# Attention and a mixture of experts on one core: score tiles in goes of six, one accumulator bank per half of d

## The chip, the cores and the metric

The kernel runs on one core of a Trainium2 chip. The core has a matrix engine (TensorE, PE in the profile, its weight loads on a row of their own, PEld), a vector engine (VectorE, DVE), a scalar engine (ScalarE, ACT), GpSimd (POOL) and SyncE (SP), which issues most transfers. TensorE writes into PSUM: eight banks, each holding 512 float32 values in each of 128 partitions. ScalarE and VectorE read the banks. The metric is the time of one execution on the device in microseconds.

## The reference

Attention without softmax over 8 batches of 2496 rows, then routing to 8 experts with a fixed capacity, then a two-layer expert network.

```python
scores = (1.0 / S) * np.matmul(z, z.transpose(0, 2, 1))   # z: 8 x 2496 x 64
attn = np.maximum(scores, 0.0) ** 2
out = u * np.matmul(attn, v)                              # u, v: 8 x 2496 x 256
x = out.reshape(B * S, D)
logits = x @ w_gate                                       # 8 experts
# (token, expert) pairs in falling order of their logit; a pair is taken
# if the token is free and the expert has room for N/8 = 2496 tokens
h = np.maximum(x[mask] @ w1[e], 0.0)                      # 256 -> 1024
out[mask] = h @ w2[e]                                     # 1024 -> 256
```

## The kernel before

**Precision.** Matmuls take float32 values as a rounded part (hi, h) and a remainder (lo, l). A product is three matmuls: hi·hi, hi·lo and lo·hi. So `zh`/`zl`, `vh`/`vl`, `hi`/`lo`, `w1h`/`w1l`, `xh`/`xl` and `hh`/`hl` are such pairs: the first part is copied by ScalarE as a rule, the remainder subtracted by VectorE.

**Attention: groups and steps.** A batch has 2496 rows: 19 key tiles of 128 and one of 64 (KT = 20). Queries are taken in five groups g of 512 columns (the last has 448). For each (batch b, group g, key tile kt) there is one step n, 800 in all (`seq`). The loop at L1016 writes out one step after another. In a step it issues, in this order: a go of scores when one is due, Relu (`rectify`, ScalarE) of the tile four steps ahead (LA = 4), square (`square`, ScalarE) of the tile two ahead, the remainder (`split_lo`, VectorE) of the next tile, the rounded part (`split_hi`; three of five on ScalarE, two on VectorE) of the tile two ahead, the output matmuls (`av`) of this step's tile, and what the table `todo` holds for this step.

**Scores.** z's columns have 64 rows, so two 64-row matmuls for two key tiles run side by side in two halves of the array, three products each (L825, the six-matmul *pair*). A *go* is the score tiles issued one after another in one step: four tiles, two pairs, at every fourth step. Each tile takes a bank of the ring `sc`, which has SCB = 4 banks. The ring also serves the transposes of z for the next batch (`z_turn`, L786, one bank, read by `zh` L792 and `zl` L793), and of the output (`turn_back`, L891, two banks, read by `post_mul` L902).

**Output.** `av` adds the products of attn and v to two banks `acc0`, `acc1`, one for each half d of v's 256 columns. Each has two buffers, so the eight banks are four for scores and four for accumulators. After a group's last tile, `take_acc` copies both into `at0` (ScalarE, L879) and `at1` (VectorE, L877) as work of the table at step m0, the next group's first. Two steps later `turn_back` turns them, one more later `post_mul` multiplies by u and stores x, and then 32 logit products (`post_logits`, L919) per group are spread on VectorE over 13 steps.

**Next batch.** z is turned 60 steps ahead of a batch, one `z_turn` every four steps; v is split (`split_v`, L806, L807) one tile per step during the last group of the batch before.

**A planner** orders each engine's instructions before the run: it takes them as written, earlier ones first, but puts a later one ahead where, by its own costs, the earlier one's inputs or buffer aren't there yet. On the chip each engine then keeps this order.

**Second stage.** Experts are taken in an order found while running; for each, a list of its 2496 rows is made (`route`, VectorE mainly), rows are gathered (`gather_x`, GpSimd), turned (`turn_x`, `xp`, L541, L550, L551) and put through both layers (L557 to L559, L588 to L590), and scattered (`put_y`, L621). An expert has 40 steps (5 groups of 8, PER = 40). While one expert is computed, the list of the next is made in pieces: `advance` is called twice a step and deals out the list's pieces evenly. With AHEAD = 10, list k starts 10 steps before expert k-1 and must be done 10 steps before expert k, when its first gather is written (list 1 starts somewhat later). Weights of an expert are split (`split_w`, L509, L511) from ten steps before it.

Of the kernel before, what the change touches and what calls it, by code (L numbers as in the profile page):

```python
# [107 lines left out]
def moe(tc, xd, first, jp, identf, w1, w2, out, B, S, cp):  # L108
# [18 lines left out]
    PLANS = ((4, 3, 3, 3, 3), (3, 3, 3, 3, 2, 2))  # L127
    ND = 15
    LA = 3
    AHEAD = 10  # L130
    YIELDS = 88
    with ExitStack() as ctx:
        rp = ctx.enter_context(tc.tile_pool(name="rp", bufs=1))
# [498 lines left out]
        def at(n, f, *a):  # L632
            todo.setdefault(n, []).append((f, a))

        for k in range(E):
            for g in range(NG):
                n0 = (k * NG + g) * FT
                at(1 if (k, g) == (0, 1) else n0 - 12 if g else n0 - AHEAD, gather_x, k, g)
                if (k, g) == (0, 0):
                    at(n0 - 6, turn_x, k, g, range(DH))  # L640
                else:
                    for d in range(DH):
                        at(n0 - 4 if (k, g) == (0, 1) else n0 - 6 + d, turn_x, k, g, (d,))
# [13 lines left out]
        steps_k = {k: 0 for k in range(E)}  # L657
        gens = {k: route(k) for k in range(1, E)}

        def advance(pos):  # L660
            k = pos // (2 * PER) + 1
            if k >= E:
                return
            skip = 2 * (AHEAD - 3) if k == 1 else 0
            if pos < skip:
                return
            want = -(-(pos % (2 * PER) - skip + 1) * YIELDS // (2 * PER - skip))
            if (pos + 1) % (2 * PER) == 0:
                want = 1000
            while steps_k[k] < want:  # L670
                w = next(gens[k], "end")
                if w == "end":
                    break
                steps_k[k] += w if isinstance(w, (int, float)) else 1
# [17 lines left out]
def attention(tc, u, v, z, w_gate, xd, identf, made, first, scale):  # L692
# [11 lines left out]
    JP = lg.shape[1]  # L704
    LA = 4
    RING = KT + 2
    SCB = 4
    with ExitStack() as ctx:
        io = ctx.enter_context(tc.tile_pool(name="io", bufs=3))
        zp = ctx.enter_context(tc.tile_pool(name="zp", bufs=2))  # L710
# [6 lines left out]
        def load_gate():  # L717
            wgb = wk.tile([128, E, D], F32, name="wgb", bufs=1)
            for h in range(2):
                wg = wk.tile([128, DH, 128 * E // 2], F32, name="wg", tag="xs")  # L720
                wg = wg.rearrange("p a b -> p (a b)")
                nc.sync.dma_start(wg, bass.AP(tensor=w_gate.tensor, offset=w_gate.offset + h * 128 * E,
                                              ap=[[0, 128], [1, 128 * E]]))
                with in_turn(0):
                    nc.vector.tensor_copy(wgb[:, :, h * 128:(h + 1) * 128], wg.rearrange("p (d e) -> p e d", e=E))
            wgt = wk.tile([128, DH, E], F32, name="wgt", bufs=1)
            nc.sync.dma_start(wgt, w_gate.rearrange("(h p) e -> p h e", h=DH))
            WG.update(rows=wgb, cols=wgt)
# [83 lines left out]
        def width(g):  # L812
            return min(512, S - 512 * g)

        def scores(n):
            b, g, kt = seq[n]
            w = width(g)
            q = slice(g * 512, g * 512 + w)
            for m in range(0, 4, 2):
                pair = [ps.tile([128, 512], F32, name="sc", bufs=SCB)[:, :w] for _ in range(2)]  # L820
                for key, query in ((ZH, ZH), (ZH, ZL), (ZL, ZH)):
                    for s in range(2):
                        r = slice(DQ * s, DQ * s + DQ)
                        k = (kt + m + s) * 128
                        nc.tensor.matmul(pair[s], key[b][r, k:k + 128], query[b][r, q],  # L825
                                         start=key is ZH and query is ZH, stop=key is ZL)
                for s in range(2):
                    SC[n + m + s] = pair[s]

        def rectify(n):  # L830
            p = SC.pop(n)
# [2 lines left out]
            R[n] = r  # L834

        def square(n):
            a = wk.tile([128, 512], F32, name="a")[:, :width(seq[n][1])]
            nc.scalar.activation(a, R.pop(n), AF.Square)  # L838
            A[n] = a

        def split_hi(n):
            h = wk.tile([128, 512], F32R, name="hi", bufs=4)[:, :width(seq[n][1])]
            if n % 5 < 3:
                nc.scalar.activation(h, A[n], AF.Copy)  # L844
            else:
                nc.vector.tensor_copy(h, A[n])
            HI[n] = h

        def split_lo(n):
            a, h = A.pop(n), HI[n]  # L850
            if seq[n][2] == NT:
                nc.vector.tensor_sub(h[TL:], a[TL:], h[TL:].bitcast(F32))
                return
            l = wk.tile([128, 512], F32R, name="lo", bufs=4)[:, :width(seq[n][1])]
            recent["l"] = nc.vector.tensor_sub(l, a, h.bitcast(F32))  # L855
            LO[n] = l

        def av(n):
            b, g, kt = seq[n]
            if kt == 0:  # L860
                ACC[b, g] = [ps.tile([128, 512], F32, name=f"acc{d}") for d in range(2)]
            last = kt == NT
            h, l = HI.pop(n), LO.pop(n, None)
            for d in range(2):
                o = ACC[b, g][d][:, :width(g)]
                c = slice(d * 128, (d + 1) * 128)
                vh, vl = VH[b, kt][:, c], VL[b, kt][:, c]
                nc.tensor.matmul(o, vh, h, start=(kt == 0), stop=False)  # L868
                if not last:
                    nc.tensor.matmul(o, vh, l, start=False, stop=False)  # L870
                nc.tensor.matmul(o, vl, h, start=False, stop=last)  # L871

        def take_acc(b, g, d):
            t = wk.tile([128, 512], F32, name=f"at{d}", bufs=2)[:, :width(g)]
            o = ACC[b, g][d][:, :width(g)]
            if d:
                nc.vector.tensor_copy(t, o)  # L877
            else:
                nc.scalar.activation(t, o, AF.Copy)  # L879
            AT[b, g, d] = t  # L880
# [12 lines left out]

        def post_mul(b, g, half):
            if half == 0:
                XS[b, g] = wk.tile([128, 4, D], F32, name="xs")
            acc = ACC[b, g][half].rearrange("p (i d) -> p i d", d=D)
            full = NT - 4 * g - 2 * half
            cuts = [(0, 2, 128)] if full >= 2 or b % 2 else [(0, full, 128), (full, 2, TL)]
            for i, j, n in cuts:  # L900
                c = slice(2 * half + i, 2 * half + j)
                nc.vector.tensor_mul(XS[b, g][:n, c], acc[:n, i:j], UR[b, g][:n, c])  # L902
            if half == 1:
                xs = XS[b, g]
                n = min(4, NT - 4 * g)
                nc.sync.dma_start(xd[b * S:b * S + NT * 128].rearrange("(p i) d -> p i d", i=NT)[:, 4 * g:4 * g + n],
                                  xs[:, :n])
                if n < 4:
                    nc.sync.dma_start(xd[b * S + NT * 128:(b + 1) * S], xs[TL * (b % 2):TL * (b % 2) + TL, n])
# [12 lines left out]
        def last_logits(b, g):  # L922
            xs = XS[b, g]
            p = ps.tile([128, 512], F32, name="sc", bufs=SCB)
            xt = [wk.tile([128, 512], F32, name="xt", tag=t, bufs=n) for t, n in (("r", 4), ("a", 3))]
            for d in range(DH):
                t = ps.tile([128, 512], F32, name="sc", bufs=SCB)
                for i in range(4):
# [22 lines left out]
        def premask(lo, hi):  # L951
            at_least(nc, first["mask0"], first["rep"], first["at0"], lo, hi)

        todo = {}

        def at(n, f, *a):
            todo.setdefault(n, []).append((f, a))
# [7 lines left out]
        for b in range(B):  # L965
            for g in range(NQ):
                n0 = (b * NQ + g) * KT
                m0 = n0 + KT
                t = m0 + (0 if m0 == B * NQ * KT else 2)
                for d in range(2):  # L970
                    at(m0, take_acc, b, g, d)
                at(t, turn_back, b, g)
                for d in range(2):
                    at(t + 1, post_mul, b, g, d)
# [9 lines left out]
            if b:  # L984
                for g in range(NQ):
                    m = n0 - 3 * KT + 4 * g
                    at(m - 4, load_z, b, g)
                    at(m, z_turn, b, g)
                    at(n0 - KT + 4 * g - 8, load_v, b, g)
                at(n0 - 3 * KT + 4 * NQ + 2, swap_z, b, slice(0, KT * 128))  # L990
                for kt in range(KT):
                    at(n0 - KT + kt, split_v, b, kt)
            else:
                for kt in range(KT):
                    at(kt - 4, split_v, 0, kt)
# [16 lines left out]
            early.enter_context(tc.issue_after(i.ins))  # L1012
        at(14, load_gate)
        N = len(seq)
        start = min(min(todo), -LA)
        for n in range(-LA, N + 4 * E):  # L1016
            if n == 2:
                early.close()
            if n % 4 == 0 and 0 <= n + LA < N:
                scores(n + LA)  # L1020
            if 0 <= n + LA < N:
                rectify(n + LA)
            if 0 <= n + 2 < N:
                square(n + 2)
            if 0 <= n + 1 < N:
                split_lo(n + 1)
            if 0 <= n + 2 < N:
                split_hi(n + 2)
            for k in sorted(k for k in todo if k < n):
# [31 lines left out]
```

## Time and profile before

| what | us |
|---|---|
| median of three runs | 2611.67 (2609.31 to 2612.87) |
| the profiled execution | 2615.43 |
| its span, first to last instruction | 2613.3 |
| attention ends (last output matmul into a bank) | about 1479 |
| first list and first gather, TensorE mostly idle | 1481 to 1560 |
| second stage, TensorE busy again | 1560 to 2614 |

The profile is of one execution. It lists for each engine the busy time, in stretches of the span too; for each group of instructions count, busy time and mean; and, in the timeline, start, duration, engine, line, operation, output<-inputs and count of merged neighbours, with the idle time before and what ended it in square brackets. A matmul's row shows its time from entering to leaving; since matmuls are pipelined the next one starts earlier. `acc<-hi,vh 128*128` is an output matmul on the whole array, `sc<-zh 64*128` a score matmul on half of it.

### The profile page before, as it was taken

To read this page: it belongs to the slowest core of one execution; us is meant where nothing else is said; L and a number is where in the kernel's file an instruction comes from. 1 tells how busy PE (TensorE), PEld (TensorE's weight loads), DVE (VectorE), ACT (ScalarE), POOL (GpSimd) and SP (SyncE) were. 2 spreads that over 40 slices of the span, in tenths; PEclk is the share of its full clock that TensorE was granted. 3 is DMA by queue.
4 is the path that set the end of the run, shared out by engine and by line. 5 is a ranking of instruction groups with operands and counts; after the bars stand their busy time and mean duration, and the time that the engine had idled before them with its cause. 6 is when DMAs were issued, how large, how long until landed. Compare 5 with 4: busy or idle time off the path is not lost.

```text
span 2613.3 us, 44527 instructions
## 1 busy us (share of the span) xinstructions
PE 2536.1 (97%) x16035; PEld 2088.6 (80%) x16035; DVE 1992.7 (76%) x6142; ACT 1521.8 (58%) x2941; POOL 381.6 (15%) x507
## 2 busy tenths in 40 slices
PE   9999999999999999999999859999999999999998
PEld 6777777777777777777777648888989889898997
DVE  6888788887898888887888768869696868686322
ACT  7788787787788887887877412323232323233332
POOL 2000000000000000000000003233333333333331
PEclk9999999999999999999999859999999999999999
DMA  4121120220221211211100011112121212122110
GB/s 139 41 79 48 51 69 32 63 73 19 61 72 39 65 48 41 80 48 51 39 32 25 16 41 46 62 47 69 42 69 43 68 45 67 46 82 63 46 42 24
DMA packets 71645, 139.60 MB, mean 53 GB/s; under 512 B 12160, under 2 KB 39680, under 8 KB 71424
## 3 DMA queue, kind: packets, MB, share of 16 engines
q1 hardware_dynamic: 56320, 95.84, 11.4%
q0 software_dynamic: 15104, 40.91, 4.9%
q8 instruction: 126, 2.06, 0.3%
q14 instruction: 95, 0.78, 0.1%
HBM read 85.60 MB, written 40.89 MB: 48 GB/s over the span
## 4 chain that ended last, share of the span: by engine, by line
PE 76%; DVE 19%; ACT 2%; issue 1%; DMA 1%; POOL 0%; POOLq 0%; DVEq 0%; ACTq 0%; SPq 0%
PE acc L868 13%; PE acc L871 12%; PE acc L870 11%; PE sc L825 11%; PE hp L557 4%; PE y L588 4%; PE y L590 4%; PE y L589 4%; PE hp L558 4%; PE hp L559 4%; DVE lt L919 3%; DVE ob L430 2%; DVE lo L855 2%; PE srch L241 2%; PE sc L891 1%
## 5 line engine op out<-in xcount | busy, mean ns | idle before, releaser
L855 DVE TENSOR_TENSOR lo<-a,hi 128x512 fp32r<-128x512 f32 (+1 forms) x760 | 512.3, 678 | 189.4 <-ACT hi L844 183.9
L868 PE MATMUL acc<-hi,vh 128*128 128x512 f32 (+1 forms) x1600 | 647.6, 405 | 1.7 <-ACT hi L844 1.7
L871 PE MATMUL acc<-hi,vl 128*128 128x512 f32 (+1 forms) x1600 | 619.0, 387 | 0.0
L870 PE MATMUL acc<-lo,vh 128*128 128x512 f32 (+1 forms) x1520 | 589.9, 388 | 0.4 <-DVE lo L855 0.2
L838 ACT ACTIVATE a<-r 128x512 f32<-128x512 f32 (+1 forms) x800 | 492.4, 632 | 146.9 <-DVE lo L855 146.8
L576 ACT ACTIVATE hh<-hp 128x512 fp32r<-128x512 f32 (+1 forms) x320 | 187.4, 586 | 542.3 <-PE hp L559 481.4
L919 DVE SCALAR_TENSOR_TENSOR lt<-xs,wgb 128x256 bf16<-128x256 f32 x1248 | 467.6, 423 | 0.5
L833 ACT ACTIVATE r<-sc 128x512 f32<-128x512 f32 (+1 forms) x800 | 426.5, 589 | 63.0 <-PE sc L825 60.8
L868 PEld LDWEIGHTS acc<-hi,vh 128*128 128x128 f32 x1600 | 301.4, 188 | 120.7 <-issue 38.9
L588 PE MATMUL y<-w2h,hh 128*128 128x256 f32 (+1 forms) x1280 | 366.4, 286 | 0.5 <-ACT y L615 0.5
L589 PE MATMUL y<-w2l,hh 128*128 128x256 f32 (+1 forms) x1280 | 363.3, 284 | 0.0
L871 PEld LDWEIGHTS acc<-hi,vl 128*128 128x128 f32 x1600 | 301.7, 189 | 57.1 <-issue 0.9
L870 PEld LDWEIGHTS acc<-lo,vh 128*128 128x128 f32 x1520 | 287.1, 189 | 50.4 <-DVE lo L855 4.7
L844 ACT ACTIVATE hi<-a 128x512 fp32r<-128x512 f32 (+1 forms) x480 | 292.3, 622 | 57.2 <-PE acc L871 55.3
L557 PE MATMUL hp<-xh,w1h 128*128 128x512 f32 (+2 forms) x646 | 265.0, 411 | 0.7 <-ACT xh L550 0.7
L558 PE MATMUL hp<-xl,w1h 128*128 128x512 f32 (+2 forms) x646 | 251.9, 390 | 0.0
L621 POOL DMA_INDIRECT out_dram<-y,idx x160 | 197.4, 1234 | 370.4 <-ACT y L615 323.4
L559 PE MATMUL hp<-xh,w1l 128*128 128x512 f32 (+2 forms) x646 | 250.7, 389 | 0.0
L588 PEld LDWEIGHTS y<-w2h,hh 128*128 128x128 f32 (+1 forms) x1280 | 241.0, 188 | 11.2 <-ACT y L615 0.9
L589 PEld LDWEIGHTS y<-w2l,hh 128*128 128x128 f32 (+1 forms) x1280 | 241.0, 188 | 9.3
L482 POOL DMA_INDIRECT xg<-xd,idx x160 | 165.2, 1033 | 387.3 <-PE xp L541 156.7
L216 POOL IOTA slot<- 128x256 bf16 x1 | 1.5, 1530 | 1454.8 <-DVE xs L902 1454.8
(1154 smaller groups left out, 3791.3 us busy)
## 6 DMA issues: line engine op xcount, KB each, us to landing
vr<-in_v_dram SPq DMA_DIRECT2D x32, 512.0 KB, 3.5
ur<-in_u_dram SPq DMA_DIRECT2D x32, 512.0 KB, 4.1
xd<-xs SPq DMA_DIRECT2D x32, 512.0 KB, 2.9
wr<-in_moe_w_dram SPq DMA_DIRECT2D x32, 512.0 KB, 5.2
zh<-zh SPq DMA_DIRECT2D x14, 320.0 KB, 3.4
zl<-zl SPq DMA_DIRECT2D x14, 320.0 KB, 5.2
zin<-in_z_dram SPq DMA_DIRECT2D x31, 128.0 KB, 2.0
vr<-in_v_dram SPq DMA_DIRECT2D x8, 384.0 KB, 3.1
```

The lines of the kernel that those rows point to most:

```text
L557: nc.tensor.matmul(p[:, c], wh, xh, start=(d == 0), stop=False)
L558: nc.tensor.matmul(p[:, c], wh, xl, start=False, stop=False)
L559: nc.tensor.matmul(p[:, c], wl, xh, start=False, stop=(d == DH - 1))
L588: nc.tensor.matmul(o, h[:, c], wh, start=first, stop=False, skip_group_check=True)
L589: nc.tensor.matmul(o, h[:, c], wl, start=False, stop=False, skip_group_check=True)
L833: recent["r"] = nc.scalar.activation(r, p, AF.Relu, scale=scale)
L838: nc.scalar.activation(a, R.pop(n), AF.Square)
L855: recent["l"] = nc.vector.tensor_sub(l, a, h.bitcast(F32))
L868: nc.tensor.matmul(o, vh, h, start=(kt == 0), stop=False)
L870: nc.tensor.matmul(o, vh, l, start=False, stop=False)
L871: nc.tensor.matmul(o, vl, h, start=False, stop=last)
L919: nc.vector.scalar_tensor_tensor(t[r], XS[b, g][r, i], 1.0, WG["rows"][r, e], op0=OP.mult, op1=OP.mult, accum_out=lg[r, j, e:e + 1])
```

## The change

- **Goes of six.** The ring `sc` has six banks (SCB = 6). The first 20 tiles are scored in goes of four, the others in goes of six.
- **One bank per half of d.** `acc0` and `acc1` have one buffer each. The first two and the last two key tiles of a group are taken together in the second's step: first both tiles' products for half 0, then both for half 1 (`av_half`). `take_acc` of half 0 now heads the step after the group's last; that of half 1 stands behind the step's `split_lo`. `turn_back` and what follows it move by one step where they would fall next to a go of scores.
- **v's splitting** for the next batch starts 18 steps ahead of it and takes 1.7 steps per tile, so that it runs over the last group and into the next batch; v's loads move with it.
- **More buffers** for `a` (3 to 5), `hi` and `lo` (4 to 6); fewer for `at0`, `at1` (2 to 1) and `xs` (3 to 2).
- **Second stage.** AHEAD is 12: lists from the third on, and the first gathers of experts from the third on, come two steps earlier. List 1 and its gather keep their steps (LATE = 2), so list 2 has 38 steps in place of 40.

```diff
-    AHEAD = 10
+    AHEAD = 12
+    LATE = 2
...
-                at(1 if (k, g) == (0, 1) else n0 - 12 if g else n0 - AHEAD, gather_x, k, g)
+                at(1 if (k, g) == (0, 1) else n0 - AHEAD + (LATE if (k, g) == (1, 0) else 0), gather_x, k, g)
...
+        starts = [None, 2 * (AHEAD - 3), 2 * (PER + LATE)] + [2 * PER * k for k in range(2, E)]
+
         def advance(pos):
-            k = pos // (2 * PER) + 1
-            if k >= E:
+            k = max([k for k in range(1, E) if starts[k] <= pos], default=0)
+            if k == 0 or pos >= 2 * PER * (E - 1):
                 return
-            skip = 2 * (AHEAD - 3) if k == 1 else 0
-            if pos < skip:
-                return
-            want = -(-(pos % (2 * PER) - skip + 1) * YIELDS // (2 * PER - skip))
-            if (pos + 1) % (2 * PER) == 0:
+            end = starts[k + 1] if k + 1 < E else 2 * PER * (E - 1)
+            want = -(-(pos - starts[k] + 1) * YIELDS // (end - starts[k]))
+            if pos + 1 == end:
                 want = 1000
...
-    SCB = 4
+    SCB = 6
...
-        def scores(n):
-            b, g, kt = seq[n]
-            w = width(g)
-            q = slice(g * 512, g * 512 + w)
-            for m in range(0, 4, 2):
+        def scores(first, count):
+            for n in range(first, first + count, 2):
+                b, g, kt = seq[n]
+                w = width(g)
+                q = slice(g * 512, g * 512 + w)
...
+        def av_half(n, d):
+            b, g, kt = seq[n]
+            last = kt == NT
+            o = ACC[b, g][d][:, :width(g)]
+            c = slice(d * 128, (d + 1) * 128)
+            h, l, vh, vl = HI[n], LO.get(n), VH[b, kt][:, c], VL[b, kt][:, c]
+            nc.tensor.matmul(o, vh, h, start=(kt == 0), stop=False)
+            if not last:
+                nc.tensor.matmul(o, vh, l, start=False, stop=False)
+            nc.tensor.matmul(o, vl, h, start=False, stop=last)
...
-                ACC[b, g] = [ps.tile([128, 512], F32, name=f"acc{d}") for d in range(2)]
...
+                ACC[b, g] = [ps.tile([128, 512], F32, name=f"acc{d}", bufs=1) for d in range(2)]
+            outer = kt < 2 or kt > KT - 3
+            if outer and kt % 2 == 0:
+                return
+            now = (n - 1, n) if outer else (n,)
             for d in range(2):
...
+                for i in now:
+                    av_half(i, d)
+            for i in now:
+                HI.pop(i), LO.pop(i, None)
...
-                for d in range(2):
-                    at(m0, take_acc, b, g, d)
+                while m0 < B * NQ * KT and (t + LA - KT) % 6 not in (1, 2, 3, 4):
+                    t += 1
+                ends[m0] = (b, g)
...
-                    at(n0 - KT + 4 * g - 8, load_v, b, g)
+                    at(n0 - KT - 6 + 7 * g, load_v, b, g)
...
-                    at(n0 - KT + kt, split_v, b, kt)
+                    at(n0 - KT + 2 + 17 * kt // 10, split_v, b, kt)
...
+        goes = {n: 4 for n in range(0, KT, 4)}
+        goes.update((n, SCB) for n in range(KT, N, SCB))
...
-            if n % 4 == 0 and 0 <= n + LA < N:
-                scores(n + LA)
+            if n in ends:
+                take_acc(*ends[n], 0)
+            if n + LA in goes:
+                scores(n + LA, goes[n + LA])
...
             if 0 <= n + 1 < N:
                 split_lo(n + 1)
+            if n in ends:
+                take_acc(*ends[n], 1)
```

More of the change, by code (lines that the diff above doesn't have):

```diff
@@ L719, in load_gate @@
             for h in range(2):
-                wg = wk.tile([128, DH, 128 * E // 2], F32, name="wg", tag="xs")
+                wg = wk.tile([128, DH, 128 * E // 2], F32, name="wg", tag="xs", bufs=2)
                 wg = wg.rearrange("p a b -> p (a b)")
@@ L823, in scores @@
                         r = slice(DQ * s, DQ * s + DQ)
-                        k = (kt + m + s) * 128
+                        k = (kt + s) * 128
                         nc.tensor.matmul(pair[s], key[b][r, k:k + 128], query[b][r, q],
@@ L827, in scores @@
                 for s in range(2):
-                    SC[n + m + s] = pair[s]
+                    SC[n + s] = pair[s]
         def rectify(n):
@@ L836, in square @@
         def square(n):
-            a = wk.tile([128, 512], F32, name="a")[:, :width(seq[n][1])]
+            a = wk.tile([128, 512], F32, name="a", bufs=5)[:, :width(seq[n][1])]
             nc.scalar.activation(a, R.pop(n), AF.Square)
@@ L841, in split_hi @@
         def split_hi(n):
-            h = wk.tile([128, 512], F32R, name="hi", bufs=4)[:, :width(seq[n][1])]
+            h = wk.tile([128, 512], F32R, name="hi", bufs=6)[:, :width(seq[n][1])]
             if n % 5 < 3:
@@ L853, in split_lo @@
                 return
-            l = wk.tile([128, 512], F32R, name="lo", bufs=4)[:, :width(seq[n][1])]
+            l = wk.tile([128, 512], F32R, name="lo", bufs=6)[:, :width(seq[n][1])]
             recent["l"] = nc.vector.tensor_sub(l, a, h.bitcast(F32))
             LO[n] = l
+        def av_half(n, d):
[8 more added lines that the diff above has]
+            nc.tensor.matmul(o, vl, h, start=False, stop=last)
         def av(n):
@@ L860, in av @@
             if kt == 0:
-                ACC[b, g] = [ps.tile([128, 512], F32, name=f"acc{d}") for d in range(2)]
-            last = kt == NT
-            h, l = HI.pop(n), LO.pop(n, None)
-            for d in range(2):
[L865 to L871, printed above, removed]
+                ACC[b, g] = [ps.tile([128, 512], F32, name=f"acc{d}", bufs=1) for d in range(2)]
[3 more added lines that the diff above has]
+            now = (n - 1, n) if outer else (n,)
+            for d in range(2):
+                for i in now:
+                    av_half(i, d)
+            for i in now:
+                HI.pop(i), LO.pop(i, None)
         def take_acc(b, g, d):
-            t = wk.tile([128, 512], F32, name=f"at{d}", bufs=2)[:, :width(g)]
+            t = wk.tile([128, 512], F32, name=f"at{d}", bufs=1)[:, :width(g)]
             o = ACC[b, g][d][:, :width(g)]
@@ L895, in post_mul @@
             if half == 0:
-                XS[b, g] = wk.tile([128, 4, D], F32, name="xs")
+                XS[b, g] = wk.tile([128, 4, D], F32, name="xs", bufs=2)
             acc = ACC[b, g][half].rearrange("p (i d) -> p i d", d=D)
@@ L924, in last_logits @@
             p = ps.tile([128, 512], F32, name="sc", bufs=SCB)
-            xt = [wk.tile([128, 512], F32, name="xt", tag=t, bufs=n) for t, n in (("r", 4), ("a", 3))]
+            xt = [wk.tile([128, 512], F32, name="xt", tag=t, bufs=n) for t, n in (("r", 4), ("a", 5))]
             for d in range(DH):
@@ L952, in premask @@
             at_least(nc, first["mask0"], first["rep"], first["at0"], lo, hi)
-        todo = {}
+        todo, ends = {}, {}
         def at(n, f, *a):
@@ L1014, in attention @@
         N = len(seq)
+        goes = {n: 4 for n in range(0, KT, 4)}
+        goes.update((n, SCB) for n in range(KT, N, SCB))
+        assert sum(goes.values()) == N
         start = min(min(todo), -LA)
```

## The prediction

> **What bounds the kernel now.** I read the engines' shares first, then the busy time by stretch, then TensorE's own timeline in the attention stage, and last the timelines of ScalarE and VectorE around the few places where TensorE starts late.
>
> ```profile
> PE 2536.1 (97%) x16035; PEld 2088.6 (80%) x16035; DVE 1992.7 (76%) x6142; ACT 1521.8 (58%) x2941; POOL 381.6 (15%) x507
> ```
>
> ```profile
> core 0: us, PE busy (x) PEld busy (x) DVE busy (x) ACT busy (x) POOL busy (x), PEclk, DMA share, GB/s
> 0.00:25.00 25.00, 18.62 (x50) 11.46 (x51) 13.33 (x57) 15.16 (x32) 15.97 (x170) 1.00 0.68 232
> 25.00:1450.00 1425.00, 1423.63 (x7308) 1091.62 (x7308) 1190.68 (x3970) 1145.12 (x2298) 1.42 (x16) 1.00 0.17 52
> ...
> 1560.00:2614.00 1054.00, 1025.98 (x8184) 929.30 (x8182) 709.65 (x1808) 332.80 (x556) 358.53 (x316) 0.99 0.16 53
> ...
> 720.80:754.50 33.70, 33.65 (x188) 27.67 (x186) 31.93 (x111) 29.72 (x70) 0.00 (x0) 1.00 0.32 97
> ```
>
> From 25 to 1450 us, attention, TensorE is busy for 1423.63 of 1425 us at the full granted clock, VectorE for 1191 (84%), ScalarE for 1145 (80%). So TensorE sets the pace, and only what shortens its own stream can shorten the stage. Only the last group of a batch, where the next v is split, is tight for another engine: VectorE is busy 31.93 of 33.70 us there.
>
> But a busy row does not say how densely TensorE works: its matmuls overlap, so I read the distance from start to start. One go of scores:
>
> ```profile
> 629.54 0.39 PE L870 MATMUL acc<-lo,vh 128*128 128x512 f32 x1
> 629.77 0.39 PE L871 MATMUL acc<-hi,vl 128*128 128x512 f32 x1
> 630.09 0.50 PE L825 MATMUL sc<-zh 64*128 64x512 f32 x2
> 630.42 0.40 PE L825 MATMUL sc<-zl,zh 64*128 64x512 f32 x2
> 630.66 0.40 PE L825 MATMUL sc<-zh,zl 64*128 64x512 f32 x2
> 630.89 0.40 PE L825 MATMUL sc<-zh 64*128 64x512 f32 x2
> 631.12 0.39 PE L825 MATMUL sc<-zl,zh 64*128 64x512 f32 x2
> 631.35 0.40 PE L825 MATMUL sc<-zh,zl 64*128 64x512 f32 x2
> 631.68 0.50 PE L868 MATMUL acc<-hi,vh 128*128 128x512 f32 x1
> 632.01 0.40 PE L870 MATMUL acc<-lo,vh 128*128 128x512 f32 x1
> 632.25 0.39 PE L871 MATMUL acc<-hi,vl 128*128 128x512 f32 x1
> ```
>
> ```profile
> L825 PE MATMUL sc<-zh x800: 362/466/793, 5.8 to 1468.7; 64*128 64x512 f32 x128, 64*128 64x448 f32 x32
> ```
>
> Each matmul lasts 0.39 us, but the next starts 0.23 us after it. Two 64-row matmuls run side by side (x2). Four distances are longer: 629.77 to 630.09 (0.32), to 630.42 (0.33), 631.35 to 631.68 (0.33) and to 632.01 (0.33). They stand where the array goes from 128*128 to 64*128 and back. Together they are 1.31 where four ordinary ones are 0.92, so one round trip costs 0.39 us. 800 score tiles in goes of four make 200 round trips, 78 us of the stage, all of it counted as busy.
>
> The Trainium skill ("Trainium Kernel Development and Optimization", section Performance Expectations) says that matmul busy time is a bad measure of closeness to the roofline, because matmuls are pipelined. By the busy row 1.4 us could be won here, by the starts up to 78; the trace agrees with the page.
>
> **The change, part by part.** *Goes of six.* The first 20 tiles keep goes of four (5 goes); the other 780 go by six (130). That is 135 round trips in place of 200, so 65 x 0.39 = **25.4 us less**. The matmuls, their columns and their weight loads stay the same in number. The cover that this needs is six free score banks at each go. The third pair starts about 1.4 us after the first, and needs the banks of tiles five and six, read by Relu one step before; the second pair of today has only 0.7 us for the same. So I cost the bigger ring at nothing. The deeper rings of a, hi and lo let ScalarE and VectorE run further ahead; nothing either.
>
> *Where TensorE waits in a go today.* Score banks also serve the turning of z (L786) and of the output (L891).
>
> ```profile
> 647.22 0.38 PE L786 MATMUL sc<-identf,zin 128*128 128x128 f32 x2
> ...
> 655.66 0.38 PE L786 MATMUL sc<-identf,zin 128*128 128x128 f32 x2
> ...
> 663.16 0.38 PE L786 MATMUL sc<-identf,zin 128*128 128x128 f32 x2
> ...
> 668.38 1.01 PE L825 MATMUL sc<-zh 64*128 64x512 f32 x2
> 668.92 0.69 PE L825 MATMUL sc<-zl,zh 64*128 64x512 f32 x2
> ...
> 669.78 0.50 PE L868 MATMUL acc<-hi,vh 128*128 128x512 f32 x1
> ...
> 761.89 0.73 PE L825 MATMUL sc<-zh 64*128 64x512 f32 x2
> ...
> 763.02 0.51 PE L868 MATMUL acc<-hi,vh 128*128 128x512 f32 x1
> ```
>
> ```profile
> 649.95 0.43 DVE L793 TENSOR_TENSOR zl<-sc,zh 64x256 fp32r<-64x256 f32 x1 [0.51 <-ACT zh L792]
> ...
> 660.07 0.43 DVE L793 TENSOR_TENSOR zl<-sc,zh 64x256 fp32r<-64x256 f32 x1 [0.17 <-ACT zh L792]
> ...
> 668.35 0.43 DVE L793 TENSOR_TENSOR zl<-sc,zh 64x256 fp32r<-64x256 f32 x1
> ```
>
> A second pair normally takes 630.89 to 631.68, 0.79 us. The one at 668.38 takes 1.40, since its bank is the one of the z turned at 663.16, and zl reads that until 668.78 (TensorE starts 0.14 us later). The one at 761.89 takes 1.13, behind the turned output. That is 0.61 and 0.34 us; I count each once in each of seven batches, **6.7 us**. In a go of six these banks come up in the third pair, 0.7 us later in the go, so I let both go.
>
> What is late next: z is turned at steps four apart, which always stood right behind a go of four. Against goes of six it falls 0, 2 or 4 steps behind one; for batch b and group g (4b + 4g + 2) mod 6, which is 4 for 12 of 35. There the third pair follows 0.13 (transposes) + 1.48 (one step of six matmuls) + 0.10 + 0.80 + 0.70 = 3.2 us after the transposes. Today's last zl ends 3.16, 4.84 and 5.62 us after them (the three pairs of rows above), and 0.14 comes on top. If these lags stay, the third pair waits 0.1, 1.8 and 2.6 us, 1.5 in the mean, 18 us over 12. If the planner, which fixes each engine's order beforehand, sees it and puts other matmuls ahead, the go is cut in two and pays one more round trip, 12 x 0.39 = 4.7. Bounds 0 to 18; I take **6**, near the cut.
>
> *One bank per half of d.* The next group may not write a bank before its copy is done.
>
> ```profile
> 643.36 0.39 PE L871 MATMUL acc<-hi,vl 128*128 128x512 f32 x1
> ...
> 752.21 0.37 PE L871 MATMUL acc<-hi,vl 128*128 128x448 f32 x1
> ```
>
> ```profile
> 644.29 0.58 ACT L879 ACTIVATE at<-acc 128x512 f32<-128x512 f32 x1
> ...
> 754.44 0.55 ACT L879 ACTIVATE at<-acc 128x448 f32<-128x448 f32 x1
> ```
>
> ```profile
> 1478.67 0.37 PE L871 MATMUL acc<-hi,vl 128*128 128x448 f32 x1
> ...
> 1479.08 0.54 ACT L879 ACTIVATE at<-acc 128x448 f32<-128x448 f32 x1 [3.60 <-PE acc L871]
> ```
>
> ```profile
> L879 ACT ACTIVATE at<-acc x39: 550/579/601, 59.6 to 1447.3; 128x512 f32<-128x512 f32 x32, 128x448 f32<-128x448 f32 x7
> L877 DVE COPY at<-acc x39: 615/685/692, 60.5 to 1448.0; 128x512 f32<-128x512 f32 x32, 128x448 f32<-128x448 f32 x7
> ```
>
> With the last two key tiles taken half by half, bank 0 is finished five matmuls before bank 1, and the next group's first two tiles are taken the same way. From the last matmul into bank 0 to the next group's first into it are then 6 x 0.23 = 1.38 us. Needed: 0.39 (the matmul) + 0.04 (1478.67 + 0.37 to 1479.08) + 0.58 (copy) + 0.14 = 1.15. For bank 1 there are 7 x 0.23 = 1.61, needed 0.39 + 0.04 + 0.69 + 0.14 = 1.26. So a copy that starts at once is hidden with 0.23 and 0.35 us to spare. Today it does not: it starts 0.54 us after the matmul's end (643.75 to 644.29), in the v-splitting group 1.86 (752.58 to 754.44), because it stands behind the step's other work. A lag L costs L - 0.27. A go falls into this gap at 13 of the 39 hand-overs and covers them; 26 are bare. Lower bound 0, upper 26 x 1.59 = 41 us, with the 0.54 everywhere 26 x 0.27 = 7. Bank 0's copy now heads its step on ScalarE and bank 1's stands behind a single lo on VectorE, so one instruction under way is the usual lag: I take 0.2 each, **5 us more**. What queues behind the waiting copy on ScalarE is the Relu, square and hi of the next step, three instructions, whose readers come after the two tiles that are ready by then; on VectorE it is a hi and the logits.
>
> The Trainium skill ("Perfetto Trace Analysis", section Optimizing Tensor Performance, Matmuls) advises that independent matmul groups rotate through different PSUM banks, so that copying one out overlaps the next group's matmuls. By that rule a bare copy, 0.04 + 0.58 + 0.14 = 0.76 us an estimate, would stand open at each of 39 hand-overs, 30 us; the rows above say that five matmuls of the other half cover it, which only the run can decide.
>
> *v's splitting over two groups.* 20 splits move from one group to about 11 in it and 9 in the next; none is added. The loads on SP's queue move with them (26, 19, 12 and 5 steps ahead of the batch and 2 after it), each behind the splits that free its buffer, so the queue is not blocked. VectorE's 31.93 of 33.70 us falls; it is worth what TensorE waited there, some tenths per batch, which I leave out. Output buffers 3 to 2, copies 2 to 1: each is reread 18 or more steps after its last reader, nothing.
>
> *The start.* The first tile's products now wait for the second's. TensorE is busy 18.62 of the first 25 us and idles anyway; 0, bounds -2 to +3.
>
> *The second stage.* From the third list on, a list and its first gather come two steps earlier; the second list has 38 steps for 40. VectorE is busy 709.65 of 1054 us, so 5% denser fits. No scatter is passed on POOL's queue: the nearest stands at step 9 before the expert, the gather goes from 10 to 12 before. One wait may change:
>
> ```profile
> 1959.40 0.66 PE L541 MATMUL xp<-identf,xg 128*128 128x128 f32 x4 [1.33 <-DVE xl L551]
> ```
>
> ```profile
> 1956.67 2.08 DVE L511 TENSOR_TENSOR w1l<-wr,w1h 128x512 fp32r<-128x512 f32 x2
> 1958.66 0.69 DVE L551 TENSOR_TENSOR xl<-xp,xh 128x512 fp32r<-128x512 f32 x1
> ```
>
> xl stands behind the weights' splitting on VectorE, which is late behind the new list's first work. With that work two steps earlier it may be gone; read once and counted for five experts, 1.33 each are 7 us. I take **3 less**, bounds -7 to +4 (the same wait met at another place).
>
> **The sum**: -25.4 - 6.7 + 6 + 5 - 3 = -24.1 us. The profiled execution took 2615.43 us (span 2613.3 and 2.1 around it), so 2591.3; the median of the three runs, 2611.67, is 3.8 lower, and there it is **2587.6 us**.
>
> **Rivals.** (a) *All covers hold*: no wait at hand-overs or z, the second stage's waits gone: -25.4 - 6.7 - 7 - 2 = -41, 2570.6. For it speaks that VectorE and ScalarE have 16 to 20% to spare. (b) *The banks eat it*: hand-overs at today's 0.54 (7) and all of z's 18, nothing from the second stage: -25.4 - 6.7 + 7 + 18 = -7, 2604.6; or the goes do not stay whole. A planner that finds a bank taken cuts a go into two, and 65 cuts would give back all 25.4, and three quarters of them leave 2605.3. (c) *Slower*: the single bank. If copies keep the 1.86 us lag, 41 us stand against 32: with z's 6, +15, 2627. It decides from a mean lag of about 1.3 us at the bare hand-overs. For it speaks that a copy can head its step and still be placed late by the planner; against, that only the v-splitting group, which the change relieves, shows such a lag.
>
> **How the numbers follow.** Forecast 0.60, (a) 0.22, (b) 0.10, (c) 0.08. A measurement can tell 0.2%, 5.2 us, from no change. Forecast and (a) are faster by more, 0.82; (b) lies at or near the border and I count it as the same, 0.10; slower 0.08. The range from 2568 to 2607 takes in (a), the forecast with its terms' ends, and the near part of (b).
>
> **What would show it.** Right: the distance from the last output matmul before a go to the first after it, less the pairs, unchanged, 135 goes of eighteen matmuls; the stage ends some 25 us earlier at the same VectorE and ScalarE busy time. Hand-over: first write to bank 0 1.4 us after the last, or later if it waits. z: third pairs longer than 0.79 us in the third group of a batch. Wrong would be goes in the timeline cut by output matmuls, or a group of 33.7 us (the row of 720.80) that does not become 33.0.

## The result, and the profile after

The kernel after takes **2644.34 us** (median of 4 runs, 2640.17 to 2647.74) against 2610.49 for the kernel before (2607.34 to 2612.87): a ratio of 1.0129, interval 1.0116 to 1.0143, so 34 us slower. The forecast was 2587.6, faster, in a range up to 2607. The sign is wrong. What came is rival (c), the single bank, whose price was given as 2627, 17 us under what was measured.

First the engines' shares on the page of the kernel after, and its chain of work that ended last:

```profile
PE 2517.1 (95%) x16035; PEld 2093.3 (79%) x16035; DVE 1992.7 (75%) x6142; ACT 1499.1 (57%) x2941; POOL 363.3 (14%) x507
...
PE 74%; DVE 14%; ACT 8%; issue 3%; DMA 2%; POOL 0%; POOLq 0%; SPq 0%; DVEq 0%; ACTq 0%
...
L865 PE MATMUL acc<-hi,vh 128*128 128x512 f32 (+1 forms) x1600 | 642.6, 403 | 36.1 <-ACT at L890 29.4
```

TensorE's busy time fell from 2536.1 to 2517.1 us, as it should if the switches of the array went away, but the time rose. The last row says where: before its output matmuls TensorE now stands idle for 36.1 us, 29.4 of them until the copy at L890 (bank 0's `take_acc` on ScalarE) releases it.

The busy time by stretch of the kernel after, with the columns of the prediction's table, first attention, then two short stretches in it:

```profile
25.00:1450.00 1425.00, 1379.23 (x7129) 1075.38 (x7129) 1163.69 (x3878) 1096.83 (x2246) 1.47 (x17) 0.99 0.17 51
315.00:325.00 10.00, 7.07 (x21) 5.11 (x21) 7.17 (x23) 6.93 (x14) 0.00 (x0) 0.66 0.01 2
878.00:890.00 12.00, 9.07 (x32) 6.55 (x30) 8.08 (x27) 8.49 (x17) 0.00 (x0) 0.72 0.00 0
```

In the same 1425 us TensorE had 1423.63 us of work and 7308 matmuls before, and 1379.23 and 7129 now. It waits for 46 us, and the two short stretches show the granted clock at 0.66 and 0.72, where the whole stage has 0.99 now and had 1.00 before. VectorE and ScalarE have less to do per us, not more: neither became the bound. Attention's last output matmul starts at 1514.29 us (1479.08 before), 35.2 us later; from there to the span's end it is 1128 us, and it was 1134. So all of the loss lies in attention.

TensorE's waits in the kernel after (releaser: us in all, times, longest):

```profile
PE acc L865 <- ACT at L890: 29.4, 26, 1.3
...
PE sc L826 <- DVE zl L794: 11.4, 8, 2.9
...
PE acc L865 <- DVE at L888: 3.0, 5, 0.9
```

None of the three stood for more than 1.0 us in the list of before (`zl` had 1.0 us there, in 6 waits, and the copies had no row). And one of its rows is gone from the list after:

```profile
PE xp L541 <- DVE xl L551: 8.1, 9, 1.3
```

Now one hand-over from the timelines of the kernel after. TensorE, then ScalarE:

```profile
247.64 0.39 PE L865 MATMUL acc<-hi,vh 128*128 128x512 f32 x1
247.87 0.40 PE L868 MATMUL acc<-hi,vl 128*128 128x512 f32 x1
248.10 0.39 PE L865 MATMUL acc<-hi,vh 128*128 128x512 f32 x1
...
249.01 0.39 PE L868 MATMUL acc<-hi,vl 128*128 128x512 f32 x1
250.72 0.50 PE L865 MATMUL acc<-hi,vh 128*128 128x512 f32 x1 [1.31 <-ACT at L890]
```

```profile
247.52 0.64 ACT L845 ACTIVATE hi<-a 128x512 fp32r<-128x512 f32 x1
248.04 0.61 ACT L834 ACTIVATE r<-sc 128x512 f32<-128x512 f32 x1
248.52 0.65 ACT L839 ACTIVATE a<-r 128x512 f32<-128x512 f32 x1
249.04 0.62 ACT L834 ACTIVATE r<-sc 128x512 f32<-128x512 f32 x1
249.52 0.66 ACT L839 ACTIVATE a<-r 128x512 f32<-128x512 f32 x1
250.04 0.63 ACT L890 ACTIVATE at<-acc 128x512 f32<-128x512 f32 x1
```

The last key tile has no `lo`, so the pair L865, L868 at 247.64 and 247.87 ends bank 0; five matmuls of bank 1 follow. Bank 0 is finished at 247.87 + 0.40 = 248.27, the copy starts at 250.04, 1.77 us later. In between ScalarE ran two Relus and two squares of later tiles without a pause. The next group's first matmul could start at 249.24 and starts at 250.72, 1.48 late. By the prediction's own rule a lag L costs L - 0.27, here 1.50: the rule holds, the lag was taken too small. Over the 39 hand-overs of this execution the median lag of bank 0's copy is 1.48 us. At the 26 that wait, the number that was called bare, it is 1.6 us in the mean; 26 x (1.6 - 0.27) is 35 us, and from start to start these hand-overs do lie 34 us above the ordinary distance. The row of 29.4 us is smaller because a row counts idle time only from a matmul's modelled end, 0.39 us after its start, while the next matmul could start after 0.23.

Why the Relus are there, as I read it: a go of six is finished as a whole, so tiles up to six ahead can be ready in their banks when the copy's step comes. The planner found the copy's input not yet finished, found later Relus and squares ready, and put them ahead. In the text of the kernel the copy heads its step; in ScalarE's order it does not.

### The profile page after: what moved, and what is told of

It is laid out like the page before. It is cut to its first block, busy times and chain, and to the rows that moved or that the text cites. A ratio compares the mean times of both kernels' runs of the same rounds, so it can differ in the third digit from the quotient of the medians.

```text
span 2642.7 us, 44224 instructions
## 1 busy us (share of the span) xinstructions
PE 2517.1 (95%) x16035; PEld 2093.3 (79%) x16035; DVE 1992.7 (75%) x6142; ACT 1499.1 (57%) x2941; POOL 363.3 (14%) x507
## 4 chain that ended last, share of the span: by engine, by line
PE 74%; DVE 14%; ACT 8%; issue 3%; DMA 2%; POOL 0%; POOLq 0%; SPq 0%; DVEq 0%; ACTq 0%
PE acc L865 11%; PE acc L868 10%; PE acc L867 10%; PE sc L826 8%; PE y L589 5%; PE hp L558 5%; PE y L591 5%; PE y L590 5%; PE hp L559 5%; PE hp L560 5%; DVE lt L930 3%; ACT r L834 3%; ACT a L839 2%; DVE lo L856 2%; PE srch L242 2%
## 5 line engine op out<-in xcount | busy, mean ns | idle before, releaser
L865 PE MATMUL acc<-hi,vh 128*128 128x512 f32 (+1 forms) x1600 | 642.6, 403 | 36.1 <-ACT at L890 29.4
L856 DVE TENSOR_TENSOR lo<-a,hi 128x512 fp32r<-128x512 f32 (+1 forms) x760 | 505.8, 673 | 224.2 <-ACT hi L845 213.5
L868 PE MATMUL acc<-hi,vl 128*128 128x512 f32 (+1 forms) x1600 | 621.2, 388 | 0.0
L834 ACT ACTIVATE r<-sc 128x512 f32<-128x512 f32 (+1 forms) x800 | 457.4, 597 | 257.7 <-PE sc L826 257.3
L930 DVE SCALAR_TENSOR_TENSOR lt<-xs,wgb 128x256 bf16<-128x256 f32 x1248 | 459.6, 416 | 0.5
L865 PEld LDWEIGHTS acc<-hi,vh 128*128 128x128 f32 x1600 | 302.1, 189 | 147.8 <-ACT at L890 39.8
L868 PEld LDWEIGHTS acc<-hi,vl 128*128 128x128 f32 x1600 | 302.1, 189 | 58.4 <-issue 1.0
L867 PEld LDWEIGHTS acc<-lo,vh 128*128 128x128 f32 x1520 | 287.8, 189 | 51.6 <-DVE lo L856 4.1
L845 ACT ACTIVATE hi<-a 128x512 fp32r<-128x512 f32 (+1 forms) x480 | 303.7, 641 | 7.6 <-PE acc L868 5.6
L622 POOL DMA_INDIRECT out_dram<-y,idx x160 | 181.4, 1134 | 383.9 <-ACT y L616 336.0
```

The source lines that it names most:

```text
L834: recent["r"] = nc.scalar.activation(r, p, AF.Relu, scale=scale)
L930: nc.vector.scalar_tensor_tensor(t[r], XS[b, g][r, i], 1.0, WG["rows"][r, e], op0=OP.mult, op1=OP.mult, accum_out=lg[r, j, e:e + 1])
```

## The experiments

Every kernel was timed beside the kernel before on the same chip, and differences are to that: 2611.02 us for the first four, 2610.17 for the next three, 2610.09 for the last two. Against it the kernel after stands at +33.9.

**1. The copy ahead of later Relus (`copy_first`).** The kernel after, but the Relus and squares of the next four steps may not be put ahead of bank 0's copy. `take_acc` returns its instruction for that.

```diff
             if n in ends:
-                take_acc(*ends[n], 0)
+                held, copy = n, take_acc(*ends[n], 0)
...
-            if 0 <= n + LA < N:
-                rectify(n + LA)
-            if 0 <= n + 2 < N:
-                square(n + 2)
+            with tc.issue_after(copy.ins) if n < held + 4 else nullcontext():
+                if 0 <= n + LA < N:
+                    rectify(n + LA)
+                if 0 <= n + 2 < N:
+                    square(n + 2)
```

> The changed kernel, but in the four steps from a hand-over on, Relu and square stand behind the copy of bank 0 on ScalarE. Theory: the planner put three Relus and two squares of later steps ahead of the copy, and that order alone makes TensorE wait (29.4 us over 26 hand-overs, 1.13 each). Then at least 22 of these 29 us go: about 2615 us, and the copy starts within 0.2 us of the last matmul's end. Rival: ScalarE has no room there, so the wait only moves to the score banks or to hi, and the time stays above 2635 us.

2605.33 us (2603.1 to 2609.29), ratio 0.9973 (0.9963 to 0.9983), -5.7: 39.5 us better than the kernel after, by the order of ScalarE's instructions alone. That is more than the 29.4 us of the row, and nearly what the distances say: the 34 us at the waiting hand-overs all but go (under 1 us is left), and the waits for bank 1's copy fall from 3.0 to 0.8 us. The timelines of `copy_first` at the same kind of place, ScalarE and then TensorE:

```profile
238.92 0.60 ACT L890 ACTIVATE at<-acc 128x512 f32<-128x512 f32 x1 [1.66 <-PE acc L868]
239.41 0.59 ACT L834 ACTIVATE r<-sc 128x512 f32<-128x512 f32 x1
```

```profile
238.48 0.40 PE L868 MATMUL acc<-hi,vl 128*128 128x512 f32 x1
...
239.63 0.39 PE L868 MATMUL acc<-hi,vl 128*128 128x512 f32 x1
239.85 0.39 PE L865 MATMUL acc<-hi,vh 128*128 128x512 f32 x1
```

ScalarE now waits 1.66 us for the bank, which costs nothing, and copies 0.04 us after the last matmul's end (238.88). The next group starts at 239.85, one ordinary distance after the last matmul. In TensorE's waits of this kernel no row for the copy at L890 is left among the long ones; what is left is z:

```profile
PE sc L826 <- DVE zl L794: 13.2, 8, 3.6
...
PE acc L867 <- DVE lo L856: 3.3, 7, 0.8
```

So one bank per half is enough where the copy is first. The Trainium skill ("Perfetto Trace Analysis", Optimizing Tensor Performance, Matmuls) advises to rotate banks between groups. The 29.4 us that the kernel after waited are near the 30 that the prediction estimated from that rule; `copy_first`, with the same banks, shows that the order and not the bank decided. That 29.4 and 30 are so near is chance: the estimate had 39 waits of 0.76 us, the trace has 26 of 1.13 in the mean.

**2. z moved (`z_moved`).** The kernel after, but the `z_turn`s that fall four steps behind a go come two steps earlier.

```diff
                     m = n0 - 3 * KT + 4 * g
+                    m -= 2 if (m + LA - KT) % 6 == 4 else 0
```

> The changed kernel, but a turning of z that falls four steps behind a go is done two steps earlier. Theory: the third pairs that wait for zl (11.4 us in 8 waits, and some 6 us at the lower clock after the two longest) go: 2627 us, no third pair of a go over 1.0 us. Rival: zl is late wherever it stands, since VectorE's logits stand ahead of it: the waits move to other goes, over 2638 us.

2632.73 us (2629.04 to 2636.5), ratio 1.0071 (1.0051 to 1.0092), +21.7: 12 us better than the kernel after. Not all that was hoped for, since some waits stayed. TensorE's waits in `z_moved`:

```profile
PE acc L865 <- ACT at L890: 30.0, 26, 1.3
...
PE sc L826 <- DVE zl L794: 5.0, 5, 1.3
```

The copies' row is that of the kernel after; the two costs are separate.

**3. Both (`both`).** The edits of 1 and 2 together.

> Both of the two edits above. Theory (the two waits are separate): the gains add up, about 2598 us, below the kernel before by 0.5%. Rival (one wait hides behind the other, or ScalarE is the bound once both go): 2610 us or more.

2595.58 us (2594.23 to 2597.85), ratio 0.9936 (0.9918 to 0.9955), -15.4. The two gains add, nearly: 39.5 + 12.1 = 51.6 off 33.9 would be -17.7, and the 2.3 us between are inside the interval. Some z waits are still there:

```profile
PE sc L826 <- DVE zl L794: 7.8, 7, 1.4
```

**4. The second stage alone (`second_alone`).** The kernel before with AHEAD = 12, LATE = 2 and the new `starts`, nothing else.

```diff
-    AHEAD = 10
+    AHEAD = 12
+    LATE = 2
...
+        starts = [None, 2 * (AHEAD - 3), 2 * (PER + LATE)] + [2 * PER * k for k in range(2, E)]
```

> The kernel before with the second stage's part of the change alone (lists and first gathers from the third on two steps earlier). Theory: the waits of xp for xl go, 6 us less, 2604 us. Rival: they move, no difference over 2 us.

2606.6 us, ratio 0.9984 (0.9973 to 0.9994), -4.4. The wait of `xp` for `xl` is gone from the long waits here too. Against that, TensorE's waits for `hx` (VectorE, in the making of the lists) rise from 10.8 us (10 waits) to 16.0 (14). From the last output matmul to the end of the span it is 1129 us, for 1134 in the kernel before. So this part of the change does what it says.

**5. Goes of two (`goes_of_two`).** The price of a round trip between 128*128 and 64*128, measured by doubling their number. The kernel before with

```diff
-            for m in range(0, 4, 2):
+            for m in range(0, 2, 2):
...
-            if n % 4 == 0 and 0 <= n + LA < N:
+            if n % 2 == 0 and 0 <= n + LA < N:
```

> The kernel before, but scores in goes of two tiles at every second step. TensorE's planned order has 408 changes from output to score matmuls and back in place of 207. Theory (a round trip costs 0.39 us and TensorE is the bound): 201 x 0.39 = 78 us more, 2689 us. Rival (the long distances overlap with something, or the trace's starts mislead): under 40 us more.

2686.3 us (2683.24 to 2687.67), ratio 1.0289 (1.0272 to 1.0307), +76.1. TensorE's order has 408 round trips where the kernel before has 207, so 76.1 / 201 = 0.379 us each; the prediction had 0.39. (With goes of two the slow second pairs of the kernel before go too, 6.9 us of which 0.4 are left; without that help it would be 82.6 / 201 = 0.41.) And the busy row does not show any of it:

```profile
25.00:1450.00 1425.00, 1425.00 (x6951) 1008.92 (x6950) 1142.10 (x3785) 1109.96 (x2199) 1.42 (x16) 1.00 0.17 51
```

TensorE is busy for 1425.00 of 1425 us, "better" than before, with 357 matmuls fewer (6951 for 7308). The count of matmuls tells the loss, the busy time hides it. The Trainium skill ("TensorEngine Tiling (Array Packing)", Key Properties) says that a change of tiling mode drains TensorE; this run agrees and gives the price, 0.38 to 0.41 us for there and back.

**6. One bank with goes of four (`four_single`).** The kernel after, with the ring of four score banks and goes of four, and still one bank per half.

```diff
-    SCB = 6
+    SCB = 4
...
-                while m0 < B * NQ * KT and (t + LA - KT) % 6 not in (1, 2, 3, 4):
+                while m0 < B * NQ * KT and (t + LA - KT) % 4 not in (1, 2):
```

> The changed kernel with goes of four and a ring of four score banks, one bank per half of d left as changed (two of the eight banks stay unused). Every hand-over then has a go of scores in it. Theory (the single bank costs only where no go covers the copy): no wait for the copies, and the time is that of the kernel before with the second stage's part alone, 2606 us, within 4 us. Rival (a single bank costs at each hand-over): 15 us or more above that, 2621 us.

2616.15 us (2613.17 to 2618.19), ratio 1.0018 (1.0008 to 1.0027), +6.0. No wait for a copy is in TensorE's list, although the copies of bank 0 are late here too: the median lag is 0.84 us, the longest 1.53. At each of the 39 hand-overs a go of scores stands before the next group's first matmul, and it covers the lag. So the single bank alone harms nothing where a go covers it, and the loss of the kernel after needs both, one bank and goes of six, which leave 26 hand-overs bare. Whether the lag is longer with goes of six (1.6 us at those) because more Relus are ready was not tried by itself. But the time is 10 us above `second_alone`, outside what was expected. Some of that is score pairs that wait for z's bank:

```profile
PE sc L826 <- DVE zl L794: 4.9, 8, 0.7
```

That is half of it. The distances from start to start give the rest: 28 goes are 0.2 to 1.1 us longer than the others of their width, 19.2 us together, where `second_alone` has 13 such goes and 6.9 us. The 12 us between the two cover the 10. Seven of them hold a wait for `zl`, three one for the turned output (`xs`); for the others the trace names no wait that explains them.

**7. z turned beside the goes of six (`z_by_six`).** `copy_first`, and z turned at every sixth step, right behind a go.

```diff
-                    m = n0 - 3 * KT + 4 * g
+                    m = n0 - 3 * KT
+                    m += 6 * g - (m + LA - KT) % 6
...
-                at(n0 - 3 * KT + 4 * NQ + 2, swap_z, b, slice(0, KT * 128))
+                at(m + 2, swap_z, b, slice(0, KT * 128))
```

> The changed kernel with the copy first, and z turned at every sixth step, always right behind a go. Theory: the third pairs' waits for zl (13.2 us in the run with the copy first, 7.8 where z was moved by two steps) all but go, 2588 us. Rival: VectorE is late there whatever the distance, 2595 us or more.

**2583.7 us** (2578.91 to 2585.52), ratio 0.9902 (0.9886 to 0.9919), -26.5: faster than both kernels. Attention by stretch, and the longest waits on TensorE in attention and on ScalarE for bank 0:

```profile
25.00:1450.00 1425.00, 1418.00 (x7444) 1121.01 (x7442) 1207.40 (x4070) 1137.48 (x2330) 1.62 (x17) 1.00 0.17 52
```

```profile
PE acc L867 <- DVE lo L856: 3.0, 7, 0.8
...
```

```profile
ACT at L890 <- PE acc L868: 44.4, 29, 2.2
```

7444 matmuls in the stretch, against 7308 before and 7129 after, at a clock of 1.00. Of z's row one wait of 0.4 us is left. ScalarE waits 44.4 us for banks to be finished, off the path. Against `copy_first` this is 20.8 us: what z's turning cost in all.

**8. v's splitting in one group again (`v_in_one_group`).** `z_by_six` with v's old steps.

```diff
-                    at(n0 - KT - 6 + 7 * g, load_v, b, g)
+                    at(n0 - KT + 4 * g - 8, load_v, b, g)
...
-                    at(n0 - KT + 2 + 17 * kt // 10, split_v, b, kt)
+                    at(n0 - KT + kt, split_v, b, kt)
```

> The fastest version so far (copy first, z turned every sixth step; 2584 us), but v split and loaded as before the change, one tile per step in a batch's last group. Theory (VectorE is full in that group, 31.93 of 33.70 us before, and TensorE now runs faster): TensorE waits there longer, 6 us or more above, 2590 us. Rival (v's place is worth nothing, as the forecast had it): within 3 us of 2584.

2586.25 us (2585.61 to 2590.01), ratio 0.991 (0.9892 to 0.9929), -23.8. The intervals overlap: spreading v is worth 2.6 us or nothing.

**9. The short rings (`short_rings`).** `z_by_six` with 3, 4 and 4 buffers for `a`, `hi` and `lo`, as before the change (and `xt`, which shares a's buffers, with them).

```diff
-            a = wk.tile([128, 512], F32, name="a", bufs=5)[:, :width(seq[n][1])]
+            a = wk.tile([128, 512], F32, name="a", bufs=3)[:, :width(seq[n][1])]
...
-            h = wk.tile([128, 512], F32R, name="hi", bufs=6)[:, :width(seq[n][1])]
+            h = wk.tile([128, 512], F32R, name="hi", bufs=4)[:, :width(seq[n][1])]
...
-            l = wk.tile([128, 512], F32R, name="lo", bufs=6)[:, :width(seq[n][1])]
+            l = wk.tile([128, 512], F32R, name="lo", bufs=4)[:, :width(seq[n][1])]
```

> The same fastest version, but the rings of a, hi and lo as before the change (3, 4 and 4 buffers). Forecast's view: the deeper rings are worth nothing, within 3 us of 2584. Rival (a go of six, and two tiles taken together, need the depth: TensorE takes no new tile for 2.3 us and then two at a time): ScalarE waits for free buffers and TensorE for hi and lo, 10 us or more above, 2594 us.

2615.36 us (2608.93 to 2616.52), ratio 1.0012 (1.0001 to 1.0022), +5.3: 31.7 us worse than `z_by_six`. The waits of TensorE, of its weight loads and of ScalarE in `short_rings`, one row of each:

```profile
PE acc L867 <- DVE lo L856: 13.0, 37, 1.5
```

```profile
PEld acc L867 <- DVE lo L856: 36.6, 64, 1.9
```

```profile
ACT a L839 <- DVE lo L856: 177.1, 212, 3.2
```

ScalarE's square waits 212 times until VectorE's `lo` frees an `a` buffer; in the kernel after, the same square waits 1.7 us in all. So ScalarE can't run ahead, and TensorE meets an unfinished `lo` 37 times instead of 7. The 13.0 us of idle time understate it, since a row counts idle only from a matmul's modelled end, 0.16 us after the next could start. From start to start, 68 distances between output matmuls are above 0.35 us in `short_rings` and 16 in `z_by_six`; they lie 31 and 9 us above the ordinary distance. That is 22 of the 31.7 us; the other 10 were not followed up. The deep rings are therefore what lets goes of six pay at all here: six banks hold the scores, but the rings hold the work made from them.

## Why the prediction was wrong

The differences put together, in us against the kernel before:

| term of the prediction | forecast | measured | by |
|---|---|---|---|
| round trips of the array | -25.4 | -24.6 (65 x 0.379; -26.7 at 0.41) | `goes_of_two` |
| second-pair waits of before | -6.7 | -6.5 (6.9 in the kernel before, 0.4 left) | distances in `z_by_six` |
| z beside goes of six | +6 (0 to 18) | +20.8, of which 12.1 by `z_moved` | `z_by_six` |
| hand-over of the banks | +5 (0 to 41) | +39.5 | `copy_first` |
| second stage | -3 (-7 to +4) | -4.4 | `second_alone` |
| v over two groups | left out | 0 to -2.6 | `v_in_one_group` |
| new short waits for `hi`, `lo` and bank 1 | nothing | +7.7 (1.7 in the kernel before, 9.4) | distances in `z_by_six` |
| sum, without v | -24.1 | +32.5 | +33.9 measured |

The rows for z and for the hand-over are differences between neighbouring runs, so they fit the total by their making. The test of the other rows is `z_by_six`, where hand-over and z are mended: -24.6 - 6.5 - 4.4 + 7.7 = -27.8 (-29.9 with the higher price of a round trip), and -26.5 was measured.

**The step that failed is the hand-over**, in these words: "Bank 0's copy now heads its step on ScalarE and bank 1's stands behind a single lo on VectorE, so one instruction under way is the usual lag". The working around it was right: the slack of 0.27 us, the rule L - 0.27, the 26 bare places, the upper bound of 41. Only the lag was read from the source's order, where it should have been read from ScalarE's. At the 26 bare hand-overs the mean lag is 1.6 us, above the point of 1.3 from which rival (c) was said to decide. The prediction knew the mechanism (a copy "can head its step and still be placed late by the planner") and gave it 0.08, on the argument that in the profile of before only the v-splitting group shows such a lag. That argument was unsound, and its reading was incomplete. In the profile of before three more hand-overs, at 424.0, 789.3 and 1154.6 us, outside the v-splitting group, have lags of 1.35 to 1.39 us; 0.54 is the median of the 39 and 0.81 the mean. And a lag read with goes of four need not hold with goes of six. What could have been worked out is an upper estimate: at a hand-over up to six tiles can be ready, each worth a Relu and a square of some 0.5 us from start to start.

**z** was on the right track and too small: 20.8 us is above its upper bound of 18, and 6 was taken. The condition (four steps behind a go, 12 of 35) and waits of about the size read hold: seven waits of 0.8 to 2.9 us stand at such goes, and one of 0.4 before them. From start to start 13 goes are longer, 17.3 us together. What was missed is that `zl` can be later than the three places that were read, and the clock. One such place in the kernel after, from TensorE's timeline:

```profile
881.32 0.76 PE L826 MATMUL sc<-zh 64*128 64x512 f32 x1 [2.93 <-DVE zl L794]
...
882.86 0.79 PE L865 MATMUL acc<-hi,vh 128*128 128x512 f32 x1
883.45 0.63 PE L867 MATMUL acc<-lo,vh 128*128 128x512 f32 x1
883.88 0.63 PE L868 MATMUL acc<-hi,vl 128*128 128x512 f32 x1
```

After 2.93 us of idle time the pair takes 1.54 us for 0.79, and the output matmuls follow at 0.43 us for 0.23, nine of them: some 2.7 us more, on top of the wait's 3. The granted clock is 0.50 from 882 to 886 us. It happens twice in the stage (the two stretches with 0.66 and 0.72 above). The long waits come from VectorE's side, in the same trace:

```profile
879.24 0.42 DVE L930 SCALAR_TENSOR_TENSOR lt<-xs,wgb 128x256 bf16<-128x256 f32 x1
...
879.70 0.42 DVE L794 TENSOR_TENSOR zl<-sc,zh 64x256 fp32r<-64x256 f32 x1
880.04 0.67 DVE L856 TENSOR_TENSOR lo<-a,hi 128x512 fp32r<-128x512 f32 x1
880.74 0.43 DVE L794 TENSOR_TENSOR zl<-sc,zh 64x256 fp32r<-64x256 f32 x1
```

The second `zl` stands behind a logit product, the first `zl` and a `lo`. It ends 6.4 us after its transposes, which start at 874.80; the three pairs of rows in the prediction had 3.2 to 5.6. The third pair came 3.2 us after them, as worked out. I took 6, near the price of a cut go; the planner did not cut these goes, they waited. It cut three others, at 178.0, 741.1 and 1302.6 us, behind their first matmul, some 1.1 us in all.

**The switches** were right, in size and in the way they were read: from start to start, not from busy time. **The second stage** was right in sign and within its bounds. **v's splitting** was rightly left out. **The deeper rings** were costed "at nothing", and as a statement that is wrong: they are worth 31.7 us once the rest is in order. It did not harm the sum, because the change contains them, but a rival in which they matter was missing. **The 6.7 us** of the second pairs were rightly read: in the kernel before 13 goes are 0.4 to 0.6 us longer than the others, 6.9 us, and in `z_by_six` three are 0.1 us longer, 0.4 us. What the prediction put at nothing, and what takes these 6.5 us back, are short waits for `hi`, `lo` and bank 1's copy: 16 distances above 0.35 us in `z_by_six`, 9.4 us, for 8 and 1.7 us in the kernel before.

## What to carry to other kernels

Where a planner sets each engine's order, a wait added to an instruction is paid in what the planner puts ahead of it: ask what else is ready on that engine at that moment, and pin the order where one bank hangs on it. Read distances from start to start where matmuls overlap, for a busy row at 100% can hide 76 us. And a longer go is only half of a change: whatever was timed to the old go (z's turning, every four steps) has to be timed to the new one. Here the pinned copy took +34 us to -6, and z timed to the new go took that to -26.

## What was not expected of the hardware

A wait of 2.93 us inside a busy stage was enough for the granted clock to halve, twice in one execution. In `copy_first` one wait of 3.59 us did so at once, and one of 3.57 us later: TensorE went on at the full pace first.

```profile
856.82 0.47 PE L826 MATMUL sc<-zh 64*128 64x512 f32 x1 [3.57 <-DVE zl L794]
...
857.67 0.50 PE L865 MATMUL acc<-hi,vh 128*128 128x512 f32 x1
858.01 0.40 PE L867 MATMUL acc<-lo,vh 128*128 128x512 f32 x1
858.24 0.59 PE L868 MATMUL acc<-hi,vl 128*128 128x512 f32 x1
858.63 0.63 PE L865 MATMUL acc<-hi,vh 128*128 128x512 f32 x1
```

The matmuls lengthen at 858.24, 1.4 us after the work came back. The Trainium skill ("TensorE: Matmul & The Clock Gate", Part 1: The HAM clock gate) says that the clock halves after an idle window of about 3.4 us which runs freely; that the change may come after the wait agrees, and the idle time of 2.93 us is shorter than that window. Single waits of up to 1.6 us, as at the hand-overs and at z's other places, show no such drop. Several short ones in a row sometimes do: in `short_rings` three waits of 0.59, 0.40 and 0.62 us between 201.7 and 204.8 us were followed by a granted clock of 0.57 from 205 to 209 us, and waits of the same size at 752 and 1303 us were not.
